# A conditioned transformer block on one core: tile and key transposes moved from the DMA engines to TensorE, paired evictions from PSUM, one memory update per segment

## The chip, the core and the metric

One NeuronCore of a Trainium2 chip runs the whole kernel. Its engines are TensorE (PE in the profile; PEld is its weight load), VectorE (DVE), ScalarE (ACT), GpSimd (POOL) and SyncE (SP). Each has an instruction stream of its own, executed in order; semaphores tie the streams together. SP issues nearly all transfers. The metric is the device time of the program in microseconds (us). Eight runs of the kernel before gave 256.39 to 261.9 us, with a median of 258.39 us.

## The reference

The input is 2048 tokens of 448 features. What is computed, cut to its core:

```python
sa, ca, ga, sb, cb, gb = (silu(c) @ w_mod) in six parts
h = layernorm(x) * (1 + ca) + sa
x = x + ga * A(h)
h = layernorm(x) * (1 + cb) + sb
x = x + gb * ((sigmoid(h @ w_gate) * (h @ w_up)) @ w_down)

def A(h):                       # 16 heads of 28, 4 segments of 512 tokens
    q, k, v = h @ wq, h @ wk, h @ wv
    M = z = 0
    for s in range(4):
        a_dot = softmax(q_s @ k_s.T * scale + causal mask) @ v_s
        a_mem = (phi(q_s) @ M) / (phi(q_s) @ z + 1e-6)
        outs.append(g * a_mem + (1 - g) * a_dot)
        M = M + phi(k_s).T @ v_s
        z = z + sum(phi(k_s))
    return concat(outs) @ wo
phi = lambda t: where(t > 0, t + 1, exp(t))
```

## The kernel before, in words

**Staging.** The tokens are four segments of 512, a segment four tiles of 128 tokens. Everything stays in SBUF between the loads and the stores. For each segment: `ln1` normalises the four tiles and brings them into the layout with the features on the partitions (`hT`, seven pieces of 64 features, each kept on both halves of the partitions); `proj` makes q, k and v; `attention` and `unit` make logits (`lg`), exponentials (`ex`), causal masks (`mask`), the product with v (`pv`) and, from the second segment on, the read of the memory; `memory` updates M and z; `wo_ln2` multiplies by wo, adds to x and normalises again; `ffn` runs gate, up and down. A `phi` of two groups of four heads is one exponential on ACT and two operations on DVE.

**The layout change.** Of the eight normalised segments (four before attention, four before the feed-forward part), three are turned on PE (`turned`: segments 0, 1 and 2 of `ln1`). The other five go through `transposed`: four DMA transposes from `xn` into `hT`, one for each tile, after which `modulated` scales and shifts the four chunks in SBUF, on DVE, ACT or POOL; two DMAs (`below`, `above`) then copy the chunks to the other half of the partitions. `memory` turns the key features in the same way: for each group of four heads one DMA transpose `pk<-pq`, then 16 small matmuls into a PSUM bank of their own, an update of `M_sb` and a masked copy `rm`. So SP issues 20 + 12 DMA transposes.

**PSUM.** There are eight banks of 512 columns. A logits group takes four of them, a gate/up job two, a q/k job two, a v job two. Each q, k or v bank is copied out by an instruction of its own (`evac`), on ACT or DVE.

**What sets the order.** `Graph.run` plans the program: it walks through time with a duration for every instruction, places on each engine the ready instruction with the highest rank plus priority (`PRM`, a table of numbers for each kind of step), and emits the instructions in that order. For steps with two or three possible engines (`evac`, masks, `aT`, `hT`) it chooses the engine. Where the plan leaves TensorE a gap, it puts dummy matmuls into a free bank (`filler`, line 1169). Loads on SP are tied: from the 13th on, a load waits for the third load before it (`DEPTH, UNTIED = 3, 13`). The order around the change is thus decided by the planner, and both orders can be listed instruction by instruction from the built programs.

**Lines.** 1125 gate/up matmuls, 1144 down matmuls, 1130 tanh, 1132 product of gate and up, 1151 output sum; 887 and 899 q/k and v matmuls, 870 and 872 their copies on ACT and DVE; 975 logits, 989 and 995 exponentials, 1002 and 1005 masks on POOL and DVE, 1034 product with v, 1041/1043 and 1058/1061 its eviction and that of the memory read, 1066 to 1088 the normalising of a unit; 607, 608, 614, 615, 620 the layer norm, 827 PE transposes, 847 and 849 their eviction, 772 DMA transposes of tiles, 784 the modulation after them, 789 and 792 the copies to the other half; 913, 914, 916 `phi`, 930 DMA transposes of key features, 938 the memory matmuls, 945, 947, 951 the update of M; 1103 wo, 1106 its sum with x; 477 all loads; 659 and 679 the matmuls on w_mod, 735 the one on beta.

Of the kernel before, what the change touches and what calls it, by code (L numbers as in the profile page):

```python
# [19 lines left out]
BACKLOG = 1e9  # L20
SLACK = 150
INF = float("inf")
# [3 lines left out]
    "ld": (-856292, -328230, -107178, -454269, -839841, -581974, -264846, -853440, 202428, -404284, -164012, 168639,  # L26
        -81911, -862286, -511637, -225270, -277300, -412442, -28961, -465045, 234125, -635918, -336194, 54463,
        -203628, -373351, -252654, 697666, 146946, -615387, -215949, -190966, 186467, 223513, 80291, -656028, 530979,
        335758),
    "ws": (-48275, -48159, -51034, -43712, -299808, -147161, -372992, 590091, -397986, -750707, 135387, -212257,  # L30
        116306, -628107, -220816, -1040875, -701983, -760934),
    "pj": (-2521967, -2328441, -2136427, -2653281, -2419801, -2585387, -2494298, -2860299, -3203214, -2808037,
        -2763437, -2246300, -2487980, -2626500, -3552082, -2610010, -2030585, -2437231, -3099081, -2772919, -2878331,
        -2770726, -3290019, -2877571, 1038223, 1465594, 1183642, 547891, 600448, 435696, 94964, 626113, 240838,
        1146906, 410946, 267240, 47058, 221996, 83360, 107533, 42963, -101413, -276269, -311881, -264618),
    "ev": (1032979, 1016905, 1453834, 1519229, 1337457, 1015529, 1364962, 1810522, 2281284, 2404639, 1287838, 2577818,
        1459558, 1041971, 1577217, 968571, 1429994, 1380742, 1162196, 1205636, 529327, 1317298, 1425001, 119643,
        -19174, 217297, 851055, 332761, -22762, -247604, 9177, -258118, 690929, 556773, 265580, 669400, -57439,
        394765, -674430, -408520, 508240, 545845, 170907, -6834, 282418, -419406, 45548, 530330),
    "ln1": (975259, 338557, 894337, 1114976, 1312849, 704987, 1938443, 997859, 676477, 993416, 783226, 1164274,  # L40
        922712, 320212, 1400181, 1388416, 1322370, 1181774, 1151209, 1092910, 757861, 261075, 846774, -82768, 133415,
        170762, 102989, 223591, 5487, 639880, -211648, -12416, -338229, -157325, 262658, 47270, 866900, -67080,
        227770, 591982, 181549, 625619, 167415, 150451, 113528, 97723, -86511, -63994, -109950, -244375, -461102,
        295398, 403, -207871, 320797, 567044, -183937, 1008369, 75268, -260416, 260035, 304593, 89983, -963022,
        -397741),
    "lg": (1062274, 1409909, 1080064, 1428750, 1398024, 1593037, 1963978, 2749073, 2484890, 1902548, 1461179, 639013,
        684895, 514033, 389759, 876153, 492531, 112963, 763167, 436571, 554437, 919463, 688882, 619029, 931868,
        432348, 727195, 162284, 543466, 1155974, 1733124, 2233501, 1880345, 1435052, 1060791, 1179532, 1203457,
        1358497, 1466512, 1477579),
    "ex": (2348378, 3011745, 2546032, 3297389, 2347173, 2958940, 3048928, 3254362, 2993947, 2485980, 1535827, 1489390,  # L50
        1675621, 1769167, 1345056, 1699302, 1806116, 822381, 1529614, 1740759, 390260, 1107675, 652642, 1466836,
        274714, 1248745, 1492252, 1189248, 1030005, 1245332, -1290878, -1387206, -2095505, -1832784, -1675071,
        -1740802, -2685663, -1975020, -1895897, -2019806),
    "mask": (1616812, 1965359, 2264988, 2472743, 1788929, 1888143, 1932408, 2007869, 2323740, 1510467, 1441277,
        1942574, 1371599, 2205626, 2018847, 1589080, 447902, 703019, 724094, 850182, 557451, -392020, -148686,
        -189570, 736629, -502031, 307506, 71100, -198575, 978047, 107268, -1364064, -616300, -198352, -183743, 217995,
        -530705, 319673, -67845, 91053, 340630, -158197, -559483, 32253, 298224, 264693, -334906, -373261, -836893,
        -270755, -1516369, -502843, -661864, -1164448, -491148, -1002675, -792104, -1227357, -458018, -747650, 1640,
        -1977181, -567070, -509543),
    "pv": (1261428, 697723, 448377, 780491, 282608, 492821, 399144, 154005, 1308987, 1299947, 904975, -239693, 751877,  # L60
        1160299, 715316, 1474185),
    "t": (3137569, 3410883, 3709453, 3708993, 3846807, 3489128, 3586175, 3669836, 3022672, 3520000, 2990897, 2566238,
        2686994, 3106365, 3639057, 2592555, 3342458, 3340649, 3570486, 2947260, 993607, 1685290, 998033, 504816,
        1069597, 1529996, 912336, 564129, 431181, 962441, 104422, 937422, 1315172, 898475, 668051, 236646, 360293,
        410329, -10014, 137723, -81728, 343634, 105959, 250544, 894267, 849731, 1783545, 1105734, 512970, 393130,
        567040, 578803, 295078, 422692, 465913, 548246, 819910, 421843, 937823, 759636, 645156, 1106733, 1222663,
        1038592, 683532, 1061725, 606435, -359811, 882727, 818905, 1544958, 899794, 626021, 1219452, 438188, 1379178,
        146880, 191684, 856351, 459465, 797062, 245641, 368649, 153718, -296908, -764911, -44872, 448424, -211812,
        242416, 303668, 17069, 338490, -65814, 406282, 43022, -130158, -390151, -518707, -2631, 74507, -482829,
        -696767, -430424),  # L70
    "mem": (-285074, -18982, 80712, 170156, 93028, -68150, 133513, 261404, 26553, -39748, 448669, -314200, 252384,
        152574, -7549, -30440, 51156, -38767, 327373, -851680, 946050, 256193, -342961, -329631, 137764, -791215,
        -265589, -161306, 406501, -425144, -183414, 313520, 89222, 40327, 84664, 256634, 395772, -22818, -249779,
        -1110954, -44623, -412000, -244757, 37687, -247365, -743354, -730077, -1124246, -348241, -678670, -965033,
        -135939, -568250, -520273, -259971, -260723, -380286, -872734, -59345, 4523, -310360, -459231, -804100,
        -557642, 210623, 400096),
    "wo": (1835804, 1782122, 1751971, 1670581, 504437, 526846, 18024, 488548, 138720, 19990, 475348, 616499, 456576,
        743185, 1320473, 911121),
    "ln2": (2084047, 2148300, 2323046, 2246819, 2226017, 2066749, 2653912, 2521336, 2420740, 1810832, 1587711,
        1802280, 1993121, 1458007, 1510853, 1848043, 1577395, 1242990, 1086437, 1298498, 1178695, 1456779, 1176298,  # L80
        1154316, 660356, 1560029, 425011, 571717, 545571, 475671, 777241, 409968, 860867, 493068, 859114, 983597,
        1193885, 1251703, 645441, 661527, 1062344, 641874, 933126, 685937, 699547, 407260, 1225509, 650967, 358967,
        1378747, 306823, 433997, 1269805, 579782, 465843, 638313, 1209156, 655049, 1475832, 1398366, 632760, 1396475,
        755750, 353021, 1024104, 1291554, 1030443, 615465, 380543, 635075, 907242, 1316750, 918347, 2178639, 1824034,
        2349983, 1258317, 1049254, 924879, 810079, 858184, 671982, 7446, 517074, 597874, 1176069, 971992, 1203777,
        632160, 1218971, 992564, 496232, 550147, 105972, 191963, -282182, -338779, -71095, -263082, -294610, -110210,
        -171405, 419592, 174953),
    "gu": (2454817, 2294452, 1519127, 1390889, 1570514, 1628323, 1906393, 1297133, 1523391, 1745738, 1654024, 1010922,
        1507850, 1192944, 1177917, 517771, 34187, 377546, 212131, 163277, 685995, 430790, 55266, 191643, 477392,
        662655, -291997, 172244, -546568, 287968, -750457, -226225, -477606, -682581, -758773, -607397, 201313, 11715,  # L90
        546325, 205602, -306294, -471465, -410558, 16382, -406503, -492869, -48821, -313511, -639853, -311731,
# [19 lines left out]
        -512096, -39818, 326929, 192740, -537426, 3326, -169075, -89915, 276705, -647462, -158452, 172805, -705456,  # L111
        164020, 822633, 125340, 549813),
}
STAY = 49219
COST = {"ACT": 1.187, "DVE": 1.016, "POOL": 0.777}


# [226 lines left out]
def kernel(  # L344
# [363 lines left out]
    def ld():  # L708
        return pr("ld", 0)
# [493 lines left out]
```

## Time and profile before

| | |
|---|---|
| median of the eight runs | 258.39 us |
| the profiled execution | 257.31 us |
| its span, first to last instruction | 255.6 us |
| mean granted TensorE clock | 0.993 |
| busy: PE, DVE, ACT, POOL | 241.2, 198.8, 146.4, 50.5 us |
| first PE matmul, last PE matmul ends | 1.2 us, 252.2 us |

The span is 1.7 us short of the profiled execution's time. Matmuls are pipelined, and a busy PE in this profile counts from the start of a matmul to its end, so the means of PE rows are longer than the distance between two starts. The distances used below are read from the timeline, which gives the start and length of each run of matmuls.

### The profile page before, as it was taken

The page shows a single profiled execution, that of the slowest core. Times are in us where ns is not written, and L with a number is a line of the kernel's source. Part 1 is how long each engine was busy: PE and PEld are TensorE (multiplying, and loading weights), DVE is VectorE, ACT ScalarE, POOL GpSimd, SP SyncE. Part 2 cuts the span into 40 slices and gives each one's busy share as a digit, 9 for nine tenths or more (in the row PEclk, how much of TensorE's full clock was granted, in tenths as well). Part 3 has the DMA queues.
Part 4 walks back from the last instruction along what each step waited for, and adds up shares of the span by engine and source line. Part 5 has one row for each costly group of instructions (what it writes and reads, how often), then busy time and mean ns, then how long its engine had stood idle before and what let it go on. Part 6 is the DMA issues. An engine that isn't in the chain of part 4 may idle for free. (4 is left out here: it accounts for less than half of the span.)

```text
span 255.6 us, 5984 instructions
## 1 busy us (share of the span) xinstructions
PE 241.2 (94%) x2404; PEld 107.2 (42%) x2404; DVE 198.8 (78%) x462; ACT 146.4 (57%) x165; POOL 50.5 (20%) x111
## 2 busy tenths in 40 slices
PE   8978969969989999999999999999999999999994
PEld 3723424434434344343334444534444544454442
DVE  4689977999989999789999998659979855242341
ACT  5048757972997787778788883359630323022310
POOL 5208041102540210036150152001211300000000
PEclk9999988999999999999999999999999999999999
DMA  5994677677234151100621032531000231100011
GB/s 154 187 207 136 179 214 185 173 179 215 59 78 86 23 113 23 21 5 16 100 76 38 0 44 41 85 76 36 4 18 18 44 83 33 54 18 3 0 38 36
DMA packets 30087, 19.78 MB, mean 77 GB/s; under 512 B 18603, under 2 KB 28524, under 8 KB 30060
## 3 DMA queue, kind: packets, MB, share of 16 engines
q1 hardware_dynamic: 29532, 18.77, 31.9%
q10 hardware_dynamic: 528, 0.63, 1.0%
q8 instruction: 19, 0.31, 0.5%
q14 instruction: 8, 0.07, 0.1%
HBM read 11.07 MB, written 1.84 MB: 50 GB/s over the span
## 5 line engine op out<-in xcount | busy, mean ns | idle before, releaser
L1125 PE MATMUL ps<-hT,wgu 64*128 64x512 bf16 x784 | 91.0, 377 | 0.5 <-DMA hT<-hT 0.4
L1130 ACT ACTIVATE tt<-ps 128x512 f32<-128x512 f32 x56 | 33.5, 598 | 60.3 <-PE ps L1125 56.5
L989 ACT ACTIVATE pT<-ps 128x2048 bf16<-128x2048 f32 x32 | 60.1, 1879 | 11.3 <-PE ps L975 10.6
L1125 PEld LDWEIGHTS <-wgu 64*128 64x128 bf16 x784 | 38.4, 94 | 46.8 <-issue 9.3
L1132 DVE SCALAR_TENSOR_TENSOR fT<-tt,ps 128x512 bf16<-128x512 f32 x56 | 38.0, 680 | 24.7 <-ACT tt L1130 24.1
L1144 PE MATMUL ps<-wd_sb,fT 128*128 128x448 bf16 x224 | 46.9, 353 | 0.0
L1002 POOL TENSOR_SCALAR_AFFINE_SELECT pT<-pT 128x512 bf16<-128x512 bf16 x33 | 21.1, 646 | 87.4 <-ACT pT L989 34.9
L887 PE MATMUL ps<-hT,wqk 64*128 64x512 bf16 x224 | 29.8, 392 | 2.0 <-DVE wqk L696 0.7
L1144 PEld LDWEIGHTS <-fT 128*128 128x128 bf16 x224 | 20.1, 98 | 23.6 <-issue 7.1
L607 DVE BATCH_NORM_STATS2 st<-x_sb 128x6 f32<-128x448 bf16 x32 | 19.6, 612 | 3.0 <-DMA x_sb<-in_A_x_dram 2.6
L887 PEld LDWEIGHTS <-wqk 64*128 64x128 bf16 x224 | 10.6, 96 | 17.1 <-issue 7.6
L615 POOL TENSOR_TENSOR rs<-rs,mhalf 128x1 f32<-128x1 f32 (+1 forms) x29 | 17.0, 587 | 2.4
L975 PE MATMUL ps<-qT,kT 28*128 28x512 bf16 (+3 forms) x256 | 16.1, 304 | 1.0 <-ACT pT L989 0.8
L995 ACT ACTIVATE pT<-ps 128x2048 bf16<-128x2048 f32 x8 | 15.0, 1877 | 2.0 <-PE ps L975 2.0
L1151 DVE TENSOR_TENSOR ot<-ps,x_sb 128x448 bf16<-128x448 f32 x16 | 9.6, 612 | 8.4 <-PE ps L1144 8.2
L1005 DVE TENSOR_TENSOR pT<-pT,cmask 128x512 bf16<-128x512 bf16 x31 | 12.0, 417 | 3.4 <-ACT pT L989 3.2
L614 POOL TENSOR_SCALAR rs<-mv 128x1 f32<-128x1 f32 (+1 forms) x29 | 6.5, 225 | 36.4 <-DVE mv L608 29.2
L1103 PE MATMUL ps<-wo_sb,oT 128*128 128x448 bf16 x64 | 13.4, 353 | 0.0
L899 PE MATMUL ps<-wvv,hT 64*128 64x448 bf16 x112 | 12.1, 350 | 0.4 <-ACT pT L989 0.3
L620 DVE TENSOR_SCALAR xn<-x_sb,mv,rs 128x448 bf16<-128x448 bf16 x32 | 11.0, 388 | 1.1 <-POOL rs L615 1.1
L1034 PE MATMUL ps<-pT,vt 128*32 128x512 bf16 (+3 forms) x256 | 11.4, 302 | 0.2 <-DVE fT L1132 0.2
L975 PEld LDWEIGHTS <-kT 28*128 28x128 bf16 x256 | 4.9, 92 | 15.6 <-issue 14.8
(99 smaller groups left out, 241.9 us busy)
## 6 DMA issues: line engine op xcount, KB each, us to landing
out_dram<-ot SPq DMA_DIRECT2D x16, 112.0 KB, 1.7
fT<-in_w_mod_dram SPq DMA_DIRECT2D x8, 196.0 KB, 2.9
wgu<-in_B_w_gate_dram SPq DMA_DIRECT2D x7, 224.0 KB, 3.5
wgu<-in_B_w_up_dram SPq DMA_DIRECT2D x7, 224.0 KB, 3.3
wd_sb<-in_B_w_down_dram SPq DMA_DIRECT2D x7, 224.0 KB, 3.7
x_sb<-in_A_x_dram SPq DMA_DIRECT2D x6, 224.0 KB, 4.2
hT<-hT SPq DMA_DIRECT2D x5, 256.0 KB, 3.2
hT<-hT SPq DMA_DIRECT2D x5, 192.0 KB, 3.3
```

The source lines that it names most:

```text
L607: nc.vector.bn_stats(st_r[:, st.at, :], src)
L615: nc.gpsimd.tensor_tensor(r, r, mhalf[:, 0:w], ALU.pow)
L887: nc.tensor.matmul(pf(b), lhsT=w, rhs=piece(hT, i, half), start=(i == 0), stop=(i == NP - 1))
L975: nc.tensor.matmul(ps[:, lg.at + hs, o:o + nq], lhsT=kT_r[r, k.at, hcs[u], kb * P:(kb + 1) * P], rhs=qT_r[r, q.at, hcs[u], kb * P:L], star ...
L989: nc.scalar.activation(pT_r[:, pTs[units[0]].at, :, w0:w0 + L], ps_, AF.Exp, scale=scale)
L995: nc.scalar.activation(dst, ps_.rearrange("p h (u w) -> p u h w", u=2), AF.Exp, scale=scale)
L1002: nc.gpsimd.affine_select(out=blk, in_=blk, compare_op=ALU.is_ge, fill=0.0, base=0, pattern=[[0, 4], [1, P]], channel_multiplier=-1)
L1103: nc.tensor.matmul(pf(b)[:, 0:D], lhsT=oT_r[:, oT.at, k, t * P:(t + 1) * P], rhs=wo_sb[:, k, :], start=(k == 0), stop=(k == NHC - 1))
L1125: nc.tensor.matmul(pf(b), lhsT=wgu[half * HR:(half + 1) * HR, chunk_of(i, half), fs], rhs=piece(hT, i, half), start=(i == 0), stop=(i == N ...
L1130: a = act(485, lambda gp=gp, tt=tt: nc.scalar.activation(tt_r[:, tt.at, :], pf(gp), AF.Tanh, scale=0.5), [n], use=[gp, tt], prio=pr("tanh" ...
L1132: f = dve(597, lambda up=up, tt=tt, ft=ft: nc.vector.scalar_tensor_tensor(fT_r[:, ft.at, :], tt_r[:, tt.at, :], 1.0, pf(up), op0=ALU.add, ...
L1144: nc.tensor.matmul(pf(b)[:, 0:D], lhsT=fT_r[:, fts[fc].at, t * P:(t + 1) * P], rhs=wd_sb[:, fc, :], start=(fc == 0), stop=(fc == NFC - 1))
```

## The change

Five parts, and a new planning of the whole program.

1. The five segments that went through DMA transposes are turned on PE (`turned_once`, four transposes a tile into two shared PSUM banks). `modulated` reads PSUM and writes SBUF, on DVE or ACT. The two copies to the other half stay DMAs.
2. Keys are turned before `phi`, on PE: eight transposes for two groups of heads into one bank. The exponential and the last step of `phi` read that bank.
3. The matmuls of the memory of a segment are one job of 64 in one bank, followed by one update of M and one masked copy.
4. q and k of one job leave PSUM in one instruction of 2 x 512 columns, two tiles of v in one of 2 x 448.
5. Loads are joined (gate and up in 8 instead of 14, down in 4 instead of 7, w_mod in whole blocks) and no longer tied; tiles 8 to 11 of x stand behind three parts of w_mod, beta stands right behind the first part. The rings `fT`, `pk` and `rm` change size.

All priorities, the costs by which the planner picks an engine, and the rule for dummy matmuls are new. In the built order the masks are split 55 on DVE and 9 on POOL (before 31 and 33), and there are 7 dummy matmuls (before 21).

```diff
-BACKLOG = 1e9
+BACKLOG = 4000
-STAY = 49219
-COST = {"ACT": 1.187, "DVE": 1.016, "POOL": 0.777}
+STAY = 145391
+COST = {"ACT": 0.829, "DVE": 0.85, "POOL": 0.804}
...
-            k = int((b.start - a.end - SLACK) // 215)
+            gap = b.start - a.end
+            k = int((gap - SLACK) // 215)
+            if k < 2 and gap > 260 and share((a.end + b.start) / 2) < 0.8:
+                k = int((gap - 45) // 215)
...
-    NXN, NH, NQ, NKT, NV, NPT, NFT = 5, 3, 3, 2, 3, 2, 17
+    NXN, NH, NQ, NKT, NV, NPT, NFT = 5, 3, 3, 2, 3, 2, 16
...
-    pk_r = ring("pk", 3, [P, TPS, P], BF16)
-    rm_r = ring("rm", 5, [P, HP], BF16)
+    pk_r = ring("pk", 2, [P, 2, TPS, P], BF16)
+    rm_r = ring("rm", 2, [P, NHC, HP], BF16)
-    DEPTH, UNTIED = 3, 13
+    DEPTH, UNTIED = 3, 999
...
-    def transposed(xn, n, hT, t, prio=0):
+    def turned_once(xn, n, hT, bs, t, prio, prev):
         def fn():
-            nc.sync.dma_start_transpose(hT_r[:, hT.at, 0:NK, t * P:(t + 1) * P], xn_r[:, xn.at, :])
+            for kc in range(NK):
+                w, c = P if kc < NK - 1 else HR, (kc % 2) * L + t * P
+                nc.tensor.transpose(pb(bs[kc // 2])[0:w, c:c + P], xn_r[:, xn.at, kc * P:kc * P + w], ident[:])
...
             def mod(e, kc=kc, r=P if kc < NK - 1 else HR):
                 v = hT_r[0:r, hT.at, kc, :]
+                x = pb(bs[kc // 2])[0:r, (kc % 2) * L:(kc % 2 + 1) * L]
...
-                    nc.scalar.activation(v, v, AF.Identity, scale=s1, bias=s0)
+                    nc.scalar.activation(v, x, AF.Identity, scale=s1, bias=s0)
-                    vec(e).tensor_scalar(v, v, s1, s0, op0=ALU.mult, op1=ALU.add)
+                    nc.vector.tensor_scalar(v, x, s1, s0, op0=ALU.mult, op1=ALU.add)
...
-            k_n[(s, hc)] = evac(lambda hc=hc: kT_r[:, k.at, hc, :], lambda bk=bk: pf(bk), [n], [bk, k], pr("ev", s))
-            q_n[(s, hc)] = evac(lambda hc=hc: qT_r[:, q.at, hc, :], lambda bq=bq: pf(bq), [n], [bq, q], pr("ev", s))
+            k_n[(s, hc)] = q_n[(s, hc)] = evac(
+                lambda hc=hc: kq_t[:, k.at:NKT + q.at + 1:NKT + q.at - k.at, hc, :], lambda bq=bq, bk=bk: pf2(bk, bq), [n],
+                [bk, bq, k, q], pr("ev", s), (840, 1130))
...
     def memory(s):
-            tr = add("SP", 1305, lambda u=hc % 2, f2=f2, pk=pk: nc.sync.dma_start_transpose(
-                pk_r[:, pk.at, :, :], pq_r[:, f2.at, u, :]), [n], take=[pk], use=[f2], move=60000, lag=3000 if s == 0 else 800, prio=pr("mem", s))
+            def turn(i=i, b=b):
+                for u in range(2):
+                    for kb in range(TPS):
+                        c = (u * TPS + kb) * P
+                        nc.tensor.transpose(pb(b)[:, c:c + P], kT_r[:, k.at, 2 * i + u, kb * P:(kb + 1) * P], ident[:])
...
+            n = act(890, lambda b=b, e=e: nc.scalar.activation(e_r[:, e.at, 0, :], pb(b), AF.Exp), [n], take=[e], use=[b],
+                    prio=pr("mem", s))
+            n = dve(335, lambda e=e: nc.vector.tensor_scalar(e_r[:, e.at, 0, :], e_r[:, e.at, 0, :], 1.0, None, op0=ALU.min), [n],
+                    use=[e], prio=pr("mem", s), lock=True)
+            made.append(dve(1100, lambda b=b, e=e, pk=pk: nc.vector.scalar_tensor_tensor(
+                pk_r[:, pk.at].rearrange("p u t k -> p (u t k)"), pb(b), 1.0, e_r[:, e.at, 0, :], op0=ALU.add, op1=ALU.max),
+                [n], take=[pk], use=[b, e], prio=pr("mem", s), lock=True))
```

## The prediction

> **What bounds the kernel now.** The page comes first. PE is busy in 94% of the span and DVE in 78%, and the chain that ended last names PE alone, but it begins only at 178 us, so an average will not do. Next come the windows, cut at 20 us, at 74 us (the first gate/up matmul, line 1125, starts at 73.97) and at 160 us.
>
> ```profile
> 0.00:20.00 20.00, 17.36 (x164) 8.86 (x166) 13.45 (x43) 7.20 (x17) 6.05 (x26) 1.00 0.93 186
> 20.00:74.00 54.00, 47.85 (x578) 21.89 (x574) 49.06 (x137) 40.23 (x43) 16.12 (x33) 0.97 0.61 158
> 74.00:160.00 86.00, 84.00 (x871) 34.55 (x872) 81.04 (x178) 66.91 (x64) 21.42 (x39) 1.00 0.23 47
> 160.00:252.00 92.00, 91.84 (x801) 41.94 (x797) 54.65 (x106) 32.07 (x43) 6.94 (x14) 1.00 0.15 37
> ```
>
> The columns are stretch, length, busy PE, PEld, DVE, ACT and POOL with counts, clock, DMA share and GB/s. From 74 us on PE has nothing left to gain but 2.2 us (2.00 + 0.16), so there every matmul added is paid in full. From 20 to 74 us PE has holes (6.2 us, and dummy matmuls besides), while DVE lacks only 4.9 us of 54: the front is DVE's. The kernel is thus two races: how soon the first gate/up matmul can start, and how much PE work lies behind it. The timeline of DVE shows what the first waits for:
>
> ```profile
> 60.84 0.62 DVE L1106 TENSOR_TENSOR x_sb<-ps,x_sb 128x448 bf16<-128x448 f32 x1
> ...
> 68.22 0.67 DVE L620 TENSOR_SCALAR xn<-x_sb,mv,rs 128x448 bf16<-128x448 bf16 x2
> ...
> 72.30 0.62 DVE L872 CAST vt<-ps 128x448 bf16<-128x448 f32 x1 [0.72 <-PE ps L899]
> ...
> 73.18 1.37 DVE L784 TENSOR_SCALAR hT<-hT,cols 128x512 bf16<-128x512 bf16 x4
> ```
>
> The last tiles are normalised at 68.9, and their modulation begins only at 73.18: between lie the DMA transposes, with 2.4 us to landing each, one after the other. The timeline of PE and the waits of SP show the second thing, late loads:
>
> ```profile
> 34.57 0.19 PE L659 MATMUL ps<-silu,fT 112*128 112x32 bf16 x1 [0.41 <-DMA fT<-in_w_mod_dram]
> 35.84 0.19 PE L659 MATMUL ps<-silu,fT 112*128 112x32 bf16 x1 [1.08 <-DMA fT<-in_w_mod_dram]
> 36.32 0.62 PE L659 MATMUL ps<-silu,fT 112*128 112x32 bf16 x13 [0.30 <-DMA fT<-in_w_mod_dram]
> 36.87 1.76 PE L887 MATMUL ps<-hT,wqk 64*128 64x512 bf16 x8
> 39.11 2.33 PE L887 MATMUL ps<-hT,wqk 64*128 64x512 bf16 x14
> 42.98 1.69 PE L887 MATMUL ps<-hT,wqk 64*128 64x512 bf16 x14
> ```
>
> After the waits for w_mod, fourteen q/k matmuls take 2.33 us instead of 1.69: the clock granted from 30 to 40 us was 0.85. SP itself had waited for tied loads:
>
> ```profile
> SPq L477 <- DMA x_sb<-in_A_x_dram: 7.6, 4, 5.9
> ```
>
> **Behind the first gate/up matmul: the price.** A run of 24 transposes (line 827) takes 1.52 us, the last of them 0.22: 57 ns a transpose. The change adds 128: 16 for each of five normalised segments and 16 for each of three memories, 7.3 us of PE. In the two built orders 48 of them stand ahead of the first gate/up matmul and 80 behind it, so 80 x 0.057 = +4.6. One v job (14 matmuls, 1.50 us) is moved behind it, +1.5, and two pieces of logits (0.33) ahead, -0.3. Of the dummy matmuls eight stood behind it and one does now: 7 x 0.216 = -1.5, which holds because the v job stands where five of them filled a gap; without that cover the gap stays open and the 1.5 is lost. Mode switches of PE are 157 and 156, no change. Sum +4.3, bounds +2.0 (the 2.2 us of holes vanish too) and +5.8 (the gaps stay). PE before ran 73.97 to 252.2, 178.2 us; I expect 182.5.
>
> The Trainium skill speaks against this change. Its page "TensorE: Matmul & The Clock Gate", section "Part 4: PE-mode transpose", gives 275 ns for such a transpose among other work and says it does not count as PE work for the clock; by its figure, as an estimate, 80 transposes would cost 22 us. The rows decide otherwise: 57 ns, and the stretch from 50 to 60 us, with 32 of them in it, was granted 1.00.
>
> **Ahead of it: the gain.** I add the mean of each row in the order in which DVE executes. Up to the third modulated chunk that is 69.9 us before and 66.5 after. Durations overlap: from 20 us to 73.9, 55.9 us of them made 49.0 busy us, a factor of 0.88. So -3.0. Nothing of this is a faster LN: DVE work that had covered the DMA transposes now stands after the chunks. The eleven small operations on beta (1.65 us of the sum, 1.4 busy) now stand ahead of 20 us, where DVE is idle for 6.5: -1.4, nothing if beta lands late. 49.0 - 4.4 = 44.6 busy us from 20 us on, plus idle time. Before that was 4.9 us. Loads that do not wait for each other: w_mod for the second norm stands ahead of all gate/up loads, so the wait of 1.8 us at line 659 and the half-clock stretch behind it should go. Against it, tiles 8 to 11 move behind 1.5 MB (0.4, 0.3 and 0.8 of w_mod and wo): at the 205 GB/s of this front they land some 7 us later, around 29 us, close to where DVE, in order, wants them, and everything queued behind that statistic would wait. I take 3.4 us of idle time, bounds 1.5 and 6. The third chunk then is there at 20 + 44.6 + 3.4 = 68.0 (66.1 to 70.6) instead of 73.9: -5.9 (-7.8 to -3.3). PE has the time: of its 74 us before that point 8.8 were holes (2.64 + 6.15) and 2.8 thirteen dummy matmuls, so 62.4, with 2.7 for 48 transposes and without the v job 63.6. The two copies to the other half (3.1 to 3.3 us) follow as before, covered by v, product and the first gate/up pieces.
>
> **What costs nothing.** DVE as a whole: 14 + 14 + 8 single copies (671, 678 and 618 ns) go, 14.4 us, and four paired ones come. Pairs: 448 columns take 618 and 512 some 675, 0.89 ns a column, so 1.13 and 1.02 us, 4.3 in all. Modulation of 17 chunks (6.9) becomes 11 at 534 ns (5.9). The last step of phi for keys reads PSUM: between the 712 ns of today and twice the 680 of line 1132; by 0.89 ns a column 1.14, so 6 x 0.42 = +2.5. The memory updates (5.1) become six operations of about 0.3 (-3.3). Six aT evictions go to ACT (-4.6), 24 masks come from POOL (+10.0 at 417 ns), two weight scalings (+0.7). Sum -5.8 of 198.8. ACT gains 16: copies +5.0, nine chunks +7.0, six aT +4.4, so 163, in a stretch (74 to 160) where it was busy 67 of 86 us. Both stay below PE. Cover gone, each microsecond in a row on DVE before 160 us would show in full.
>
> **Sum.** -5.9 + 4.3 = -1.6. Span 255.6 to 254.0, profiled execution 257.3 to 255.7, and the median, which lay 1.1 above that execution, 256.8. Own range of this case: -5.8 to +2.5, 252.6 to 260.9.
>
> **The rivals.** *Slower: the front does not move.* DVE's list is only as short as its waits. If x tiles 8 to 11 or beta land after DVE reaches them, its queue stands, and the first gate/up stays at 74: then only the price is left, 258.4 + 4.3 = 262.7. The balance tips at a start of 69.7 us; over 72.3 it is slower by more than 1%. For it: DVE had 4.9 us of idle time despite a full list, and the load of x is moved behind 1.5 MB. Against: the wait for the transposes is real, and gone.
>
> *Slower by banks.* Turned tiles hold two of eight banks from the first tile to the last chunk, a turned key pair one until DVE's 1.14 us are done. If gate/up, which needs two, finds only two free while logits hold four, each job waits for tanh and product, 0.60 + 0.68: in five segments with two such jobs 12.8 us, 258.4 - 1.6 + 12.8 = 269.6. It decides from about three such jobs on. Against: the single dummy matmul behind the start says that the order has hardly a planned gap.
>
> *Faster in both.* Idle time of DVE at its lower bound (-7.8) and PE without holes (+2.0): 252.6.
>
> *That it does not do what it says*: the built order has no DMA transpose left, so this is out.
>
> **How the numbers follow.** 1% is about what a measurement of this kernel can tell from no change; that puts the borders at 255.8 and 261.0. My case has 0.55, spread from 252.6 to 260.9 about 256.8; the faster rival 0.18, the front that does not move 0.17, the banks 0.10. Faster by over 1%: 0.18 and somewhat under half of mine, 0.44. Slower: 0.24 of the two rivals and a trace of mine, 0.25. Within: 0.31. The range 251.5 to 262.5 leaves out most of the banks' case and a part of the two others.
>
> **What would show it.** The first line-1162 matmul at 66 to 71 us; PE from there to its end 180 to 184 us; the rows of transposes 80 and 48 at about 57 ns apart; no wait for w_mod near 35 us and no clock below 0.95 after 20 us; DVE near 193 busy us, ACT near 163; DVE idle 20 us to the start under 6 us. A start after 72.3 would make me wrong at the front; PE holes over 6 us after the start, behind it.

## The result and the profile after

The changed kernel takes 270.17 us (median of 22 runs, 268.63 to 272.53), the kernel before 257.68 beside it (62 runs, 254.14 to 261.9): a ratio of 1.0527, 95% interval 1.0504 to 1.055. It is 5% slower, outside the predicted range. The span of the profiled execution is 269.7 us where it was 255.6.

First the windows of the changed kernel, cut at 20 us, at its own first gate/up matmul (79.4) and at 160; columns as before.

```profile
0.00:20.00 20.00, 16.18 (x152) 8.39 (x153) 14.10 (x46) 7.18 (x16) 5.37 (x24) 1.00 0.93 197
20.00:79.40 59.40, 49.16 (x623) 24.72 (x620) 46.30 (x120) 46.81 (x38) 12.30 (x28) 0.97 0.57 122
79.40:160.00 80.60, 79.65 (x901) 36.88 (x898) 74.07 (x160) 63.56 (x65) 5.81 (x12) 1.00 0.09 24
160.00:267.00 107.00, 104.71 (x852) 45.64 (x848) 60.26 (x117) 44.57 (x56) 7.62 (x18) 1.00 0.07 22
sum 267.00, PE 249.70 PEld 115.63 DVE 194.72 ACT 162.12 POOL 31.09; mean PE 62.42 PEld 28.91 DVE 48.68 ACT 40.53 POOL 7.77
```

The totals are as predicted: DVE 194.7 busy us (193 expected), ACT 162.1 (163). In the second window, however, every engine has room at once. DVE is idle for 13.1 of 59.4 us, PE for 10.2, ACT for 12.6, and the DMA share is lower than it was. Nobody is the bound; they wait for each other. The first gate/up matmul starts at 79.46 instead of 73.97 (+5.5), and from there to the start of the last down matmul it is 186.5 us instead of 177.9 (+8.7).

The timeline of PE, DVE and ACT shows who waits for whom. Start, length, engine, line, operation; in brackets the idle time before and the releaser that the profile infers.

```profile
18.23 1.01 ACT L886 CAST kT<-ps 128x1024 bf16<-128x1024 f32 x1 [0.89 <-PE ps L903]
19.29 1.24 PE L903 MATMUL ps<-hT,wqk 64*128 64x512 bf16 x9 [0.90 <-ACT kT L886]
...
24.22 0.91 ACT L886 CAST vt<-ps 128x896 bf16<-128x896 f32 x1 [0.87 <-PE ps L903]
25.18 0.39 PE L903 MATMUL ps<-hT,wqk 64*128 64x512 bf16 x2 [0.97 <-ACT vt L886]
...
25.83 1.90 PE L903 MATMUL ps<-hT,wqk 64*128 64x512 bf16 x16
...
27.84 1.23 DVE L888 CAST kT<-ps 128x1024 bf16<-128x1024 f32 x1 [3.72 <-ACT pT L1025]
...
29.12 1.50 PE L916 MATMUL ps<-wvv,hT 64*128 64x448 bf16 x14 [1.39 <-DVE kT L888]
...
30.66 1.01 ACT L886 CAST kT<-ps 128x1024 bf16<-128x1024 f32 x1 [2.83 <-PE ps L916]
...
32.53 1.67 PE L841 MATMUL ps<-ident,xn 128*128 128x128 bf16 x27 [1.58 <-ACT vt L886]
33.25 1.04 DVE L861 TENSOR_SCALAR hT<-ps,cols 128x512 bf16<-128x512 bf16 x2 [2.70 <-PE ps L841]
```

Read it as a chain. At 27.84 DVE begins to copy a pair of sums that lie in banks 4 and 6, and stands 3.72 us before. The bracket names an exponential, which that copy does not read. The sums were complete at 26.22. What ended 0.11 us before the copy began is the q/k job in banks 5 and 7 (its 14 matmuls are the rear of the row at 25.83; they end at 27.73). In the built program the copy indeed waits for the count that PE reaches with the last matmul of that other job. At 29.12 PE, in order, waits for the copy; at 30.66 the next copy on ACT, of banks 5 and 7, complete since 27.73, waits for the v job in banks 4 and 6 until 30.62; at 32.53 PE waits for ACT. The copy reads its two banks as one access with a stride, and when the program is built its waits are set for the box around it, with every bank between. As the pairs of the front lie in banks 4 and 6 and in 5 and 7 by turns, each pair waits for the next one; at 19.29 and 25.18 it is PE that waits so, for copies that have nothing to do with its job. Comparing each start with the end of the last work that truly shares an element with it, such waits come to about 14 us ahead of the first gate/up matmul, on three engines and partly side by side, and to 3.1 us behind it.

Two smaller things stand in the timeline of PE. The beta matmul, first in PE's queue, waits for its load, and the transposes of the first tiles behind it:

```profile
9.40 0.17 PE L742 MATMUL ps<-beta_row,ones 1*128 1x16 bf16 x1 [1.27 <-DMA beta_row<-in_A_beta_dram]
9.50 1.13 PE L841 MATMUL ps<-ident,xn 128*128 128x128 bf16 x13
```

And a run of 16 tile transposes is three times as long as one of 8 key transposes, not twice:

```profile
75.62 0.62 PE L950 MATMUL ps<-ident,kT 128*128 128x128 bf16 x8
76.35 1.84 PE L782 MATMUL ps<-ident,xn 128*128 128x128 bf16 x16
78.13 1.50 PE L916 MATMUL ps<-wvv,hT 64*128 64x448 bf16 x14
```

Between the starts of the single matmuls lie 56 ns among the keys. In the tile rows it is 56, 56, 149 and 176, 0.44 us for the four of a tile instead of 0.22: the fourth turns only 64 columns and is issued in another shape of the array, and both changes of shape cost. That it is the change and not the 64 columns could be read in the profile before: line 827 has rows of such transposes there, and within them two start 3 ns apart and the next two mostly 53 ns later; only where a row of 128 columns goes over into one of 64, and back, lie 149 and 151 to 176 ns. The Trainium skill, "TensorEngine Tiling (Array Packing)", section "Key Properties", says that changing the tiling mode drains TensorE; the 149 and 176 ns agree. It was the rule to look up here.

One number comes from the kernel, not from the chip. The scheduler that writes the order has a start and an end for every job, and its two plans end at the same moment, 246.9 us: it expected nothing from the change as a whole. PE's first gate/up matmul ran 5.8 us behind its plan before and 14.2 us behind it in the changed kernel, the last job 6.3 and 20.5. So the question is not what the new order is worth but what its plan does not know.

### The profile page after: what moved, and what is told of

It reads as the page before. It is cut to its first block, busy times and chain, and to the rows that moved or that the text cites. A ratio compares the mean times of both kernels' runs of the same rounds, so it can differ in the third digit from the quotient of the medians.

```text
span 269.7 us, 6070 instructions
## 1 busy us (share of the span) xinstructions
PE 249.7 (93%) x2518; PEld 115.6 (43%) x2518; DVE 194.7 (72%) x440; ACT 162.1 (60%) x174; POOL 31.1 (12%) x82
## 3 DMA queue, kind: packets, MB, share of 16 engines
HBM read 11.07 MB, written 1.84 MB: 48 GB/s over the span
## 4 chain that ended last, share of the span: by engine, by line
PE 63%; DVE 18%; ACT 10%; DMA 4%; issue 3%; SPq 1%; DVEq 0%; ACTq 0%
PE ps L1162 26%; PE ps L1181 13%; PE ps L903 5%; PE ps L916 4%; ACT pT L1025 3%; DVE st L622 3%; PE ps L782 3%; PE ps L1070 3%; PE ps L1011 3%; DMA beta_row<-in_A_beta_dram 3%; ACT kT L886 2%; PE ps L1140 2%; DVE hT L861 2%; DVE fT L1169 2%; DMA hT<-hT 2%
## 5 line engine op out<-in xcount | busy, mean ns | idle before, releaser
L1162 PE MATMUL ps<-hT,wgu 64*128 64x512 bf16 x784 | 92.7, 377 | 0.7 <-DVE fT L1169 0.3
L1167 ACT ACTIVATE tt<-ps 128x512 f32<-128x512 f32 x56 | 33.5, 598 | 52.9 <-PE ps L1162 52.4
L1162 PEld LDWEIGHTS <-wgu 64*128 64x128 bf16 x784 | 39.0, 94 | 46.5 <-issue 10.6
L903 PE MATMUL ps<-hT,wqk 64*128 64x512 bf16 x224 | 28.4, 378 | 4.1 <-ACT kT L886 1.9
L1041 DVE TENSOR_TENSOR pT<-pT,cmask 128x512 bf16<-128x512 bf16 x55 | 21.1, 412 | 6.4 <-ACT pT L1025 5.3
L886 ACT CAST kT<-ps 128x1024 bf16<-128x1024 f32 x14 | 14.1, 1013 | 9.4 <-PE ps L903 5.5
L903 PEld LDWEIGHTS <-wqk 64*128 64x128 bf16 x224 | 11.2, 94 | 17.4 <-issue 6.7
L1011 PE MATMUL ps<-kT 28*128 28x512 bf16 (+3 forms) x256 | 16.2, 305 | 0.1
L1070 PE MATMUL ps<-pT,vt 128*32 128x512 bf16 (+3 forms) x256 | 12.0, 312 | 3.1 <-ACT vt L886 1.0
L916 PE MATMUL ps<-wvv,hT 64*128 64x448 bf16 x112 | 12.6, 368 | 1.4 <-DVE kT L888 1.4
L1102 DVE STREAM_TRANSPOSE A<-aT 128x512 uint32<-128x512 uint32 (+1 forms) x16 | 10.1, 637 | 1.8 <-ACT aT L1094 1.6
## 6 DMA issues: line engine op xcount, KB each, us to landing
wgu<-in_B_w_gate_dram SPq DMA_DIRECT2D x3, 448.0 KB, 12.6
```

Source lines behind the costliest of these rows:

```text
L886: nc.scalar.copy(dst(), src())
L903: nc.tensor.matmul(ps[:, b, :], lhsT=w, rhs=piece(hT, i, half), start=(i == 0), stop=(i == NP - 1))
L916: nc.tensor.matmul(ps[:, b, 0:D], lhsT=piece(hT, i, half)[:, (t + half) * P:(t + half + 1) * P], rhs=wvv[half * HR:(half + 1) * HR, chunk_ ...
L1011: nc.tensor.matmul(ps[:, lg.at + hs, o:o + nq], lhsT=kT_r[r, k.at, hcs[u], kb * P:(kb + 1) * P], rhs=qT_r[r, q.at, hcs[u], kb * P:L], star ...
L1041: nc.vector.tensor_tensor(blk, blk, cmask[:].rearrange("p (o k) -> p o k", o=1).to_broadcast([P, 4, P]), ALU.mult)
L1070: nc.tensor.matmul(pf(acc)[hs * HP:(hs + 1) * HP, kb * P:L], lhsT=vt_r[:, v.at, kb, hc * 4 + hs, :], rhs=pT_r[:, pT.at, hs, OFF[kb]:OFF[kb ...
```

## The experiments

Theory A: the boxes around paired copies tie jobs together that share nothing. Theory B: the pair itself, two banks on one long instruction. Theory C: the changes of shape in the tile transposes. Beta's load is a fourth, small cost.

**Banks 5 and 6 exchanged.** Nothing else is changed, after the plan is made:

```diff
+        slots = {id(s): s for n in order for s in n.take if s.pool == "bank" and s.width == 1}
+        for s in slots.values():
+            s.at = {5: 6, 6: 5}.get(s.at, s.at)
```

> Same instructions in the same order on every engine; only the names of PSUM banks 5 and 6 are exchanged wherever a tile has one bank. Theory A (the box): a paired copy reads two banks with a stride, and waits are set as if it touched every bank between them; in the changed kernel the pairs of the front are banks 4 and 6 and banks 5 and 7, so each covers a bank of the next pair. At 27.84 us the copy on DVE starts 0.11 us after a q/k job in banks 5 and 7 ended, although it reads 4 and 6, which were done at 26.22. With 5 and 6 exchanged most pairs of the front are neighbours (4 and 5, 6 and 7). A expects the waits of 1.2, 1.1, 1.3, 1.5, 2.8 us between 19 and 31 us to go, the first gate/up matmul at 73 to 76 us instead of 79.5, the time at 263 to 267 us (before 257.7, the changed kernel 270.2). Theory B (the pair itself): two banks hang on one longer instruction, 1.01 us on ACT and 1.23 on DVE, behind the exponentials; nothing of that depends on bank names, so B expects 269 to 271.5 us and the first gate/up matmul at 79 to 80.

Measured: 261.21 us, ratio to before 1.015 (1.0093 to 1.0207), 9.0 less than the changed kernel. The first gate/up matmul is at 69.58, 9.9 earlier; a part of that is beta's load, which was in time in this profile (its first transposes stand 1.25 us earlier). The gain is larger than A had put it. The same jobs in its timeline:

```profile
22.22 1.99 PE L906 MATMUL ps<-hT,wqk 64*128 64x512 bf16 x16
...
22.65 1.22 DVE L891 CAST kT<-ps 128x1024 bf16<-128x1024 f32 x1 [1.01 <-PE ps L906]
...
24.02 1.50 PE L919 MATMUL ps<-wvv,hT 64*128 64x448 bf16 x14
24.24 1.01 ACT L889 CAST kT<-ps 128x1024 bf16<-128x1024 f32 x1
...
25.79 1.96 PE L844 MATMUL ps<-ident,xn 128*128 128x128 bf16 x32
...
26.52 1.95 DVE L864 TENSOR_SCALAR hT<-ps,cols 128x512 bf16<-128x512 bf16 x4 [1.17 <-ACT vt L889]
```

The copy on DVE now runs beside the q/k job instead of behind it, and PE's brackets are gone. B has no place for that: the pairs are as long as before.

**Copies split.** Each pair leaves PSUM in two instructions again, at the same place in the order:

```diff
...
-                lambda hc=hc: kq_t[:, k.at:NKT + q.at + 1:NKT + q.at - k.at, hc, :], lambda bq=bq, bk=bk: pf2(bk, bq), [n],
+                lambda hc=hc: [kT_r[:, k.at, hc, :], qT_r[:, q.at, hc, :]],
+                lambda bq=bq, bk=bk: [ps[:, lesser(bk, bq), :], ps[:, greater(bk, bq), :]], [n],
...
```

> The same order, but each of the 24 paired copies is issued as two, one for each bank. A (the box) expects the same waits to go as by exchanged banks, all of them this time, and to pay for 24 more instructions: 0.34 us each (0.68 twice against 1.01), 20 on ACT and 4 on DVE, of which about 18 stand ahead of the first gate/up matmul: that at 73.5 to 76.5 us, the time at 263 to 268 us. B (the pair) expects that the first bank is free a third of a microsecond sooner and the second as much later: no gain worth the name, 269 to 272 us.

Measured: 260.21 us, ratio 1.0104 (1.0043 to 1.0164); first gate/up matmul at 70.17, and 184.2 us behind it, 2.4 less than in the changed kernel. 24 more instructions, and still 10 us faster than the pairs; this too is more than A had put it. The boxes behind the start, which the exchange of 5 and 6 left as they were (186.2 us), are gone here.

**Beta early.** Its load is issued third on SP's queue:

```diff
+        order.remove(self.beta)
+        order.insert(order.index(self.c) + 1, self.beta)
...
```

> The load of beta (32 bytes) is issued third on SP's queue, right after c, instead of behind the loads of x and the weights; nothing else is changed. In the changed kernel PE stands from 7.9 to 9.40 us for the beta matmul, in front of the first transposes. If that wait is on the path of the front: first transposes at 7.9 to 8.2 us, the first gate/up matmul 1.2 to 1.6 us earlier than 79.5, the time at 268.4 to 269.2 us. If later waits of the front swallow it: 269.8 to 270.5 us.

Measured: 269.26 us, 0.9 less and between the two ranges; the first transposes at 7.99, the first gate/up matmul at 77.37, 2.1 earlier than in the profile of the changed kernel. The wait in that profile is not in every execution: with the load at its place in the changed kernel, the profiles of the two runs above and of the next have the beta matmul at 8.14, 7.26 and 7.70, without a wait for DMA. So the median shows less than one profile does. Nor is the 0.9 beta's alone. The four executions here had a mean granted clock of 1.00. Of the 22 of the changed kernel twelve had 0.998 or more, with a median of 269.4 us, and ten had 0.987 to 0.994, with a median of 271.1. At the same clock beta's place is worth 0.2 us; whether its late load brings the lower clock about is not shown.

**The fourth transpose 128 wide.** The last 64 columns are zeros:

```diff
-                w, c = P if kc < NK - 1 else HR, (kc % 2) * L + t * P
+                w, c = P, (kc % 2) * L + t * P
```

> The fourth transpose of each normalised tile takes 128 columns (the last 64 are zeros, their rows are not read) instead of 64; the same count of instructions. In the changed kernel the groups of four take 56 + 56 + 149 + 176 ns to the next matmul, 0.44 us, where eight equal transposes of keys stand 56 ns apart. Theory C: the change of shape is what costs, twice in each tile; then 20 tiles give back 20 x 0.21 = 4.3 us of PE, 16 of them (3.5 us) behind the first gate/up matmul, where PE has no holes: 266 to 267.5 us, and PE from that matmul to its end 186.5 minus 3 to 3.5 us. Rival: the 149 and 176 ns are latency in which the array is free anyway, or the time is waited for elsewhere: 269.5 to 270.5 us.

Measured: 266.21 us, 4.0 less (3.2 less than the twelve executions at the full clock, as these four were), and in the timeline of PE 16 of them take 1.05 instead of 1.84 us:

```profile
73.30 0.62 PE L950 MATMUL ps<-ident,kT 128*128 128x128 bf16 x8
74.04 1.05 PE L782 MATMUL ps<-ident,xn 128*128 128x128 bf16 x16
```

C holds: transposing more columns is cheaper. From the first gate/up matmul to the last down matmul it is 184.2 us, 2.1 less than in the run before, not 3.5: some of what the shapes cost had been waited for anyway.

**All three, and neighbours.** The first of the next two adds up the edits; the second also exchanges banks 5 and 6 and splits only copies whose banks are not neighbours.

> The three edits together: copies split, beta loaded early, fourth transpose 128 wide. If the three costs are separate they add up: 270.2 minus 10.0 (split), minus 0.9 (beta), minus 4.0 (wide) = 255.3 us, range 254.5 to 256.5, first gate/up matmul near 69.4 us and 182 us from it to the end. If one hides behind the other (PE's holes are filled either way): 257 to 259 us.

Measured: 256.41 us, ratio 0.9982 (0.9945 to 1.0018). The first gate/up matmul is at 68.93, with 182.5 us behind it. The three costs are separate and add up to within 1.1 us; taken from the 269.4 of the full clock they are 9.2, 0.2 and 3.2, and add up to within 0.4.

> As the one before, but banks 5 and 6 exchanged and a copy split only where its two banks are no neighbours; neighbours keep the paired copy. Theory A: a pair without a bank between costs nothing by itself and saves 0.34 us of ACT each, so the front gains a little over splitting all (69.6 against 70.2 in the two runs made): 254 to 256 us, first gate/up matmul 68.5 to 69.5. If pairs cost something even as neighbours (B, weaker): 256 to 258 us.

Measured: 256.22 us, ratio 0.999 (0.9948 to 1.0031); first gate/up matmul at 67.96, and 182.05 us behind it. The time lies 0.2 above A's range and in B's, the start earlier than A's. Against splitting all, pairs as neighbours cost nothing that can be seen; that they gain is not shown either (0.2 us). Its windows:

```profile
0.00:20.00 20.00, 18.16 (x173) 9.34 (x175) 14.88 (x50) 9.00 (x19) 6.38 (x27) 1.00 0.96 220
20.00:67.90 47.90, 43.76 (x602) 22.79 (x598) 44.98 (x118) 44.57 (x38) 11.37 (x26) 1.00 0.62 142
67.90:160.00 92.10, 91.30 (x1027) 41.20 (x1023) 84.11 (x183) 72.14 (x76) 9.48 (x20) 1.00 0.08 22
160.00:250.40 90.40, 89.75 (x728) 39.30 (x722) 48.99 (x93) 36.31 (x48) 3.94 (x10) 1.00 0.09 25
```

DVE is idle for 2.9 us of the second window (13.1 before the repair), the clock is 1.00, and PE has 1.45 us of holes behind the start. This is the change as it was meant, and by its median it is level with the kernel before.

The clock is not the same in the two. Of the 45 executions of the kernel before that were taken beside these experiments only three had a mean granted clock of 0.998 or more; they took 254.50 to 255.66 us. The others had 0.974 to 0.993. Eight of the ten here had 0.998 or more, with a median of 256.2. So at the full clock the change as it was meant is some 1.6 us slower, by three executions, and it is level because the kernel before loses more to the clock.

**Tile transposes twice.** The price of a transpose by itself, on the kernel just shown:

```diff
-            for kc in range(NK):
+            for kc in [*range(NK), *range(NK)]:
```

> As e6, but the four transposes of each of the 20 normalised tiles are issued twice: 80 more transposes, 64 of them behind the first gate/up matmul, where PE has no holes. At 56 ns each, the pitch in the rows of equal shapes: +3.6 us behind it, +3.6 to 4.6 us in all. At 275 ns each, the figure of the Trainium skill's page TensorE: Matmul & The Clock Gate (Part 4), it would be an estimated +17.6 us.

Measured: 259.68 us, 3.5 more, just under the range, and in its timeline of PE

```profile
66.69 1.95 PE L790 MATMUL ps<-ident,xn 128*128 128x128 bf16 x32
```

for what had been 1.06 us with 16: 56 ns each more. Behind the start it is 2.5 us more and not 3.6: PE's holes there shrink from 1.45 to 0.5 us. The rest is ahead of it; part of that is a later tile of x (first transposes at 9.24 instead of 8.04). The 275 ns of the Trainium skill's page "TensorE: Matmul & The Clock Gate" (Part 4) do not hold for runs of one shape.

**The loads alone.** The kernel of before, without the waits of loads for each other; its order is unchanged:

```diff
-            if n.tie is not None:
+            if n.tie is not None and False:
```

> The kernel of before, in which the loads do not wait for the load three places ahead of them; its order is as it was. It tells what the part of the change on loads is worth alone. The wait of PE for w_mod (0.41 + 1.08 + 0.30 us at 34.6 to 36.3) and the slow clock behind it (2.33 instead of 1.69 us) should go in any case. If the front is DVE's, as the prediction had it, the time stays: 257 to 258.3 us. If PE's wait was on the path: 255.3 to 256.5 us.

Measured: 256.41 us, ratio 0.9984 (0.9931 to 1.0038): not told from no change. The wait for w_mod is gone and the first gate/up matmul is at 72.77, 1.2 earlier. That the slow clock would go was wrong. Half the clock was granted from 33.5 to 40.3 us in this profile, and from 37.1 to 40.4 in that of the kernel before; fourteen matmuls take 1.48 us longer for it instead of 0.64. The gap of 0.66 us lies inside that stretch and did not start it:

```profile
34.44 1.49 PE L887 MATMUL ps<-hT,wqk 64*128 64x512 bf16 x6 [0.66 <-DVE hT L847]
...
36.40 3.17 PE L887 MATMUL ps<-hT,wqk 64*128 64x512 bf16 x14
```

**Each transpose where its engine is free.** What the runs say is that turning on PE is paid behind the start, where PE has few holes and DMA a share of 0.08. (What it gives ahead of the start, beside the other parts of the change, was not run by itself.) So the tiles behind the start go back to DMA transposes:

```diff
+    DMA_LN1, DMA_LN2 = (3,), (1, 2, 3)
...
+            if s in DMA_LN2:
+                trs.append(transposed(xn, ln, hT, t, pr("ln2", s)))
```

The priorities were searched anew, so the whole order differs; the second run is the same with 12 instead of 16 tiles, the third a control with the search alone.

> As e6, but the 16 normalised tiles that are turned behind the first gate/up matmul (third segment's attention input, and the second norm of segments 1 to 3) go by DMA as in the kernel of before, and only what stands ahead of it (4 such tiles, and the keys) is turned on TensorE. The order was searched anew with the kernel's own scheduler, whose plan for it ends 3.7 us sooner (243.1 for 246.9). If PE behind the first gate/up matmul is what is paid (64 transposes x 56 ns = 3.6 us, and DMA has a share of 0.07 there): PE from that matmul to its end 178 to 180 us instead of 182.05, the time 252 to 254 us, faster than both kernels. Rival: the wait for landings (2.4 us each) comes back into PE's way, as it does in the plan without a new search (260 us): 255.5 to 258 us.

Measured: 250.68 us, ratio 0.9745 (0.971 to 0.978). It is faster than both kernels, also than the kernel before at the full clock (254.50 to 255.66), and better than expected: first gate/up matmul at 68.09, and 177.0 us behind it.

```profile
67.90:160.00 92.10, 90.56 (x1035) 39.75 (x1031) 82.17 (x177) 73.50 (x78) 11.68 (x22) 1.00 0.16 36
160.00:246.00 86.00, 85.42 (x665) 38.00 (x653) 50.62 (x100) 30.08 (x40) 7.27 (x16) 1.00 0.14 36
```

PE's holes are 2.1 us instead of 1.45 although landings of 2.4 us are back: little of their latency shows, and PE has 64 transposes fewer.

> As the one before, but only the second norm of segments 1 to 3 (12 tiles, 48 transposes) goes by DMA; its plan ends at 243.6. By 56 ns each 2.7 us come back: 252.5 to 254.5 us; by the rival 255.5 to 258.

Measured: 252.85 us, ratio 0.983 (0.979 to 0.9869); 179.3 us behind the start.

> The control for the two: e6 with nothing but an order searched anew in the same way (plan 246.4 instead of 246.9). If the gain of the two comes from PE's work and not from the search, this one stays within 0.6 us of e6's 256.2: 255.2 to 256.6 us. If the search is what helps, it gains as much as they do.

Measured: 254.7 us, ratio 0.9905 (0.9868 to 0.9943); 180.6 us behind the start. The control gained 1.5 us, more than its expectation allows, so the search is a part of the gain. Beyond it the DMA transposes bring 1.9 us with 12 tiles and 4.0 with 16, by 56 ns each 2.7 and 3.6. Each of the three has an order of its own, so how much of a difference is its order and how much its transposes is not told apart more finely than this.

## Why the prediction was wrong

**The step that failed** is the one on paired copies, in the part headed "what costs nothing". They were costed by their duration on DVE, 1.13 us for q and k, and that size was near (1.23). What one instruction over two banks waits for, and who then waits for it, was not asked; of the front the prediction said that PE "has the time". The runs put in its place: 9 to 10 us (8.2 and 9.2 at the same clock) for boxes that cover a neighbour's bank, 7 to 8 us of it ahead of the first gate/up matmul (77.37 with beta early against 69.58 and 70.17) and up to 2.4 behind. None of the rivals was this. "Banks" named too few banks for gate/up; here banks were free and waits were set on them. Its number, 269.6, is right by accident.

**57 ns a transpose** came from a run of 24 of one shape and was applied to 80 that are not. For keys it holds. The tiles took 0.44 us for four, 110 ns each, and the runs price that at 3.2 to 4.0 us over the whole kernel, 2.1 behind the start. Doubling them shows that 57 is right where the shape stays. The prediction had asked the right question and counted wrong: "157 and 156, no change" leaves out the switches inside the groups of a tile. Counted by the array shape of successive matmuls in the built programs there are 177 before and 215 after, and 179 with the fourth transpose 128 wide.

**"Nothing if beta lands late"** was the wrong floor. The beta matmul stands in PE's queue ahead of the first transposes, so a late beta costs: 1.27 us in one profile. In the median it is 0.9 us at most and 0.2 at the same clock, for in three of the four profiles with the load at that place beta is in time.

**What was right.** Without these three the two terms come out as written. The front: 68.0 expected, 67.96 in the run with neighbours; DVE from 20 us on 44.6 busy and 3.4 idle expected, 44.98 and 2.9 measured. The price behind it: +4.3 expected, 182.05 against 177.9 is +4.2. The time then is 256.2 to 256.4 for 256.8. These are the totals. The parts of the front's term (the order on DVE, beta's small operations, the loads) were not run one by one; the ties of the loads alone bring 1.2 us at the start and nothing that can be told in the time. The price is the outcome of 4.9 us more work and 0.7 us of holes that closed, and the prediction's sum left the holes open. So some of the agreement may be luck. One count in the prediction is wrong, though its sum is not: 14.4 us is that of 7 + 7 + 8 single copies on DVE, not of 14 + 14 + 8. The sum was made of the work and of the waits that the data needs; it had no term for waits between jobs that share nothing.

**Other signs.** No wait for w_mod near 35 us: right. No clock below 0.95: wrong, from 50 to 60 us 0.83 was granted, with a gap of 0.88 us in it; in the run with neighbours it is 1.00. DVE idle under 6 us: wrong, 13.1. PE 180 to 184 us behind the start: wrong, 186.5. PE's holes there are 3.2 us, under the 6 that were to tell.

**Left open.** How early PE begins differs from execution to execution by up to 1.7 us (first transposes at 7.8 to 9.5 us). Where beta is loaded third, the fourth tile of x is what came late in several profiles; it did so once where beta is not (0.88 us in that of the split copies). Which place of the load is best was not tried.

## What to carry to other kernels

One instruction over two places that are not neighbours can be made to wait for everything between them: choose neighbours, or issue two. When all engines have idle time in the same window, look for waits between jobs that share no data; compare each start with the end of the last work that truly touches its operands, since the releaser in brackets may be a bystander that ended at the same moment. And an operation moved to an engine is worth its saving only where that engine has holes: the best kernel here turns its tiles on PE ahead of the start and by DMA behind it.

## What the runs showed of the hardware

A transpose of 64 columns among such of 128 makes both gaps around it longer, 149 and 176 ns instead of 56; padding it with zeros to 128 halves the time of the four, from 0.44 to 0.22 us. And 24 more copies on busy engines cost less than the waits of 24 pairs: 260.2 against 270.2 us.
